# Whole 128x128 products outside column tiling, a narrower memory update, and a newly planned order in a two-layer attention and GEGLU kernel

## The chip, the cores and the metric

The kernel runs on one core of one Trainium2 chip. A core has five engines that work side by side: PE (matrix products, with its weight loads shown apart as PEld), ACT (activations), DVE (vector), POOL (GpSimd) and SP (here it only issues transfers). The metric is the device time of one execution in microseconds, as a median over runs.

## The reference

Two layers, each an attention block with a compressive memory followed by a GEGLU block, with the same weights in both layers. x is 2048 x 512, 32 heads of 16, four segments of 512 rows, hidden width 1792, all bf16.

```python
x = x + _A_ref(_layernorm(x), wq, wk, wv, wo, beta)
x = x + _B_ref(_layernorm(x), w_gate, w_up, w_down)     # and both once more

# _A_ref, for each segment s in order (q, k, v of that segment; M, z start at zero)
logits = einsum('bhqd,bhkd->bhqk', qs, ks) * scale + mask      # causal within the segment
a_dot = einsum('bhqk,bhkd->bhqd', softmax(logits), vs)
pq = phi(qs)                                                   # phi(t) = t + 1 if t > 0 else exp(t)
num = einsum('bhld,bhde->bhle', pq, M)
den = einsum('bhld,bhd->bhl', pq, z)[..., None] + 1e-06
o = g * num / den + (1.0 - g) * a_dot                          # g = sigmoid(beta), per head
M = M + einsum('bhld,bhle->bhde', phi(ks), vs)
z = z + einsum('bhld->bhd', phi(ks))
# ... then o @ wo

# _B_ref
gelu(x @ w_gate) * (x @ w_up) @ w_down
```

## The kernel before, in words

**Work.** There are eight rounds k = 0 to 7: four segments of the first layer, then four of the second. A round normalizes its 512 rows (bn_stats on DVE, the scale on POOL, xn on DVE) and turns them to xnT, by a DMA transpose, or on PE through "ident" for a few tiles (`turn_item`). Then PE makes q, k and v; the scores; the products of the exponentials with the values; the memory terms; the output projection (wo); and the three GEGLU products (wg_sb, wu_sb, wd_sb). Everything PE writes goes to one PSUM tile, `big`, of eight banks of 512 columns. A "product" is one contraction over 128 rows, of up to 512 columns, into 128 output partitions.

**Modes of the array.** PE's array is used in three ways. *Rows*: the scores, four instructions side by side that each contract over 32 partitions (a head's 16, or 32 with the other half zeroed) and write four banks (L1422). *Columns*: four instructions side by side that each contract over 128 partitions and write 32 output partitions. The products of exponentials (`pt`) and values (`vaug`, `vS`) use it because the four heads have different data (L1118), and before the change every other product after the start uses it too, with the same moving data four times (`product`, L655). *Whole*: one instruction over the full array; before the change only the first warm-up products (L553) and the first transposes (L753) are whole. Each instruction is a weight load and a matmul, so a product is eight instructions in columns and two as a whole.

**A score step** is four banks of scores (`visit`), one ACT exponential over the four (`pt`, L1492), causal masks on POOL (L1465), and later a *flush*: the products of `pt` and values in column mode, whose result DVE transposes, divides and transposes back (L1146 to L1161). There are 145 steps. For the first 64 keys and queries of each 128-row diagonal tile a shared form, `kS` (L817) and `vS` (a transfer on SP, L889), packs two heads into one tile.

**Memory.** phi(q) and phi(k) come from an exponential on ACT and two steps on DVE (L923 to L957); phi(k) is turned by a DMA transpose (`phik<-e`). The update (`upd_item`) sums phik x vaug over the segment's four tiles for four blocks of eight heads: 16 products of 128 columns, into a 128 x 128 block per eight heads, of which only the eight 16 x 16 diagonal blocks are M. DVE adds that to `macc` and multiplies it with the block mask `bd` into `mblk` (L1057, L1073). The reading products are `zcols,phiq` (8 columns, the denominator) and `mblk,phiq` (128 columns, the numerator); the quotient `am` goes back by a DMA transpose (`amT<-am`).

**GEGLU.** The gate's result goes to `gel` either through ACT's GELU straight from PSUM, or for the first RAW of the 14 tiles as a copy, on which ACT then runs GELU over GELU_TILES tiles at once (L1274). DVE multiplies with the up product (L1309); the down product is added to x on DVE (L1219). Rounds 0 and 7 treat their rows in two halves, so that their gate and up products are 256 columns wide.

**The order.** The order of every engine is fixed when the program is built. A loop at the end of the kernel holds clocks for all engines (`Clocks`, with a cost per product, 0.108 us for a change of mode, and a simple clock for the loads) and picks, step by step, a score step, a flush, the next product of an open item, or, if nothing is ready, a filler product on `warm` whose result is not read. Which item comes first follows from due times and slacks, in tables of numbers (`DUE`, `BIAS`, `TUNING`, `CHANGES`, the last by stretches of 8 us). On the chip each engine runs its list in order and waits with semaphores, so a late instruction holds all that is listed behind it on that engine.

Of the kernel before, what the change touches and what calls it, by code (L numbers as in the profile page):

```python
# [36 lines left out]
V_FIRST = -0.1406  # L37
WG_GAP, WU_GAP, WD_GAP = 1.1751, 1.964, 2.2
# [7 lines left out]
HALF_DUE = -0.0614  # L46
# [4 lines left out]
WO, WG, X2, WU, X3, WD = 8.92, 8.8357, 9.3414, 26.0, 59.6338, 50.0  # L51
# [3 lines left out]
GELU_TILES = 2  # L55
RAW = 7
QK_DUE = 0.6083
E_Q = -0.5755
E_K = 1.0635


PIECE_SLACK = 2.4403
# [14 lines left out]
DUE = {"wo": 0.9072, "gate": 1.0383, "up": 1.341, "down": 2.1385, "upd": 0.3142, "mem": -0.0606, "v": -0.0049}  # L77
DUE_STEP = {"gate": 0.0081, "up": 0.0201, "down": 0.0554}
BIAS = {
    **{("qk", k): d for k, d in {0: 0.6366, 1: -0.4157, 2: 0.0872, 3: 0.0468, 4: 0.1308, 5: -0.6926, 6: 0.341, 7: 0.1923}.items()},  # L80
    **{("mem", k): d for k, d in {0: -0.207, 1: -0.081, 2: -0.1962, 3: 0.5227, 4: 0.8136, 5: -0.0693, 6: -0.6952, 7: 0.185}.items()},
    **{("down", k): d for k, d in {0: 0.3399, 1: 0.5019, 2: -0.0456, 3: -0.5138, 4: -0.6002, 5: 0.0995, 6: -0.0146, 7: -0.2413}.items()},
    **{("upd", k): d for k, d in {0: 1.4259, 1: 0.8971, 2: -0.1168, 3: 1.283, 4: -0.1814, 5: 0.6044, 6: 0.1034, 7: 1.0768}.items()},
    **{("v", k): d for k, d in {0: -0.3587, 1: 0.46, 2: -0.4336, 3: 2.2572, 4: -0.1536, 5: -1.113, 6: -0.5383, 7: 0.1758}.items()},
    **{("wo", k): d for k, d in {0: -0.1308, 1: 0.6124, 2: -1.1607, 3: -0.6612, 4: -0.5868, 5: -1.3174, 6: 0.2871, 7: -0.2375}.items()},
    **{("gate", k): d for k, d in {0: 0.5854, 1: -0.059, 2: -0.7641, 3: -0.6794, 4: -0.8448, 5: 0.349, 6: -0.5712, 7: -0.7185}.items()},
    **{("up", k): d for k, d in {0: -0.2823, 1: 0.018, 2: -0.1402, 3: -0.3188, 4: -0.0282, 5: -0.0777, 6: -0.2846, 7: 0.3301}.items()},
# [5 lines left out]
    8.0: {"ADD": -17.428, "AHEAD": -0.005, "CAP": 5, "DIRECT": -14.575, "EAGER": 1, "EXP_SLACK": -5.116, "FIRST": -12.912, "FLUSH_WAIT": 9.26, "KB_FIRST": 1.044, "KB_SLACK": 5.078, "KS_FIRST": 3.677, "PHI_SLACK": 9.086, "SCALES": -12.366, "SOON": 0.419, "TURNED": -10.958, "X_NORM": 0.107, "down": -0.264, "gate": -0.13, "qk": -0.178, "up": 0.131, "upd": -0.423, "v": 0.893, "wo": -0.005},  # L93
    16.0: {"ACT_EVICT": -1.716, "ADD": -15.287, "AHEAD": 0.315, "CAP_FREE": 4, "EXP_SLACK": -2.291, "E_SLACK": 11.836, "GELU_SLACK": 0.422, "H_NORM": -12.256, "KB_SLACK": 0.3, "KS_SLACK": 8.888, "MASK_STEP": 0.443, "PHI_SLACK": 3.266, "QUAD": 1, "SCALES": -14.004, "X_NORM": 0.549, "gate": -0.366, "mem": 0.376, "qk": 0.34, "up": -0.311, "upd": -0.413, "v": -0.056},
    24.0: {"ACT_EVICT": 1.44, "CAP_FREE": 4, "DIRECT": -15.128, "EAGER": 1, "E_SLACK": 10.283, "FIRST": -12.109, "FLUSH_WAIT": 14.141, "GELU_SLACK": -0.282, "H_NORM": -13.364, "KB_SLACK": 0.694, "KS_SLACK": 5.286, "PHI_SLACK": 0.4, "SOON": 0.354, "X_NORM": 0.705, "down": 0.382, "gate": -0.53, "mem": 0.434, "qk": 0.414, "v": 0.047, "wo": 0.796},
    32.0: {"ACT_EVICT": 1.686, "ADD": -13.497, "AHEAD": 0.174, "CAP": 3, "CAP_FREE": 6, "EAGER": 0, "EXP_SLACK": 0.685, "E_SLACK": 11.451, "FLUSH_WAIT": 13.243, "GELU_SLACK": -0.725, "KB_FIRST": -1.682, "KS_FIRST": 10.752, "MASK_STEP": 0.471, "MEM_SLACK": 2.767, "PHI_SLACK": 1.429, "QUAD": 0, "SCALES": -12.323, "TURNED": -9.789, "X_NORM": 0.549, "down": 0.592, "gate": -0.755, "mem": -0.285, "wo": -0.005},
    40.0: {"ACT_EVICT": 2.537, "AHEAD": 0.152, "DIRECT": -15.882, "EXP_SLACK": -2.179, "E_SLACK": 12.429, "FLUSH_WAIT": 14.141, "GELU_SLACK": -0.767, "H_NORM": -13.609, "KB_SLACK": 1.429, "KS_FIRST": 6.764, "MEM_SLACK": 2.596, "PHI_SLACK": 4.309, "QUAD": 1, "SCALES": -14.004, "X_NORM": 0.622, "mem": -0.479, "qk": -0.3, "upd": -0.012, "wo": 1.011},
    48.0: {"AHEAD": -0.043, "CAP": 5, "CAP_FREE": 4, "DIRECT": -17.12, "FIRST": -10.627, "GELU_SLACK": 0.029, "KB_SLACK": 0.694, "KS_FIRST": 11.509, "MASK_STEP": 0.139, "MEM_SLACK": 4.617, "PHI_SLACK": 4.307, "QUAD": 1, "SCALES": -14.713, "SOON": 0.173, "mem": -0.412, "qk": -0.299, "upd": -0.805, "v": 0.391},
    56.0: {"ACT_EVICT": 3.045, "ADD": -13.348, "EXP_SLACK": -2.607, "E_SLACK": 11.451, "FIRST": -8.214, "FLUSH_WAIT": 10.746, "GELU_SLACK": -0.767, "KS_FIRST": 13.703, "MASK_STEP": 0.327, "MEM_SLACK": 4.065, "PHI_SLACK": 3.783, "QUAD": 1, "SOON": 0.293, "TURNED": -10.962, "X_NORM": -2.154, "down": 0.561, "gate": -0.36, "mem": -0.457, "qk": -0.363, "up": 0.131, "upd": -1.138, "v": 0.541, "wo": -0.786},
    64.0: {"ACT_EVICT": 1.495, "ADD": -13.677, "AHEAD": 0.164, "KB_SLACK": 1.66, "KS_FIRST": 12.054, "KS_SLACK": 6.956, "MASK_STEP": 0.416, "MEM_SLACK": 4.617, "PHI_SLACK": 12.047, "QUAD": 0, "SCALES": -14.004, "SOON": 0.507, "TURNED": -9.034, "X_NORM": 0.0, "down": 1.162, "gate": -0.726, "upd": -1.362, "v": -0.146, "wo": -1.126},  # L100
    72.0: {"ACT_EVICT": 1.417, "CAP": 5, "CAP_FREE": 6, "EAGER": 0, "EXP_SLACK": -6.38, "E_SLACK": 9.522, "FIRST": -7.036, "H_NORM": -13.913, "KB_FIRST": -1.775, "KB_SLACK": 0.777, "KS_FIRST": 15.351, "MASK_STEP": 0.22, "MEM_SLACK": 5.407, "SCALES": -11.012, "SOON": -0.293, "mem": -0.412, "v": 0.004, "wo": 0.934},
# [57 lines left out]
    536.0: {"AHEAD": 0.262, "FLUSH_WAIT": 8.259, "PHI_SLACK": 3.033, "X_NORM": 0.605, "gate": 0.339, "v": -0.058},  # L159
    544.0: {"ADD": -9.41, "CAP": 5, "DIRECT": -10.972, "H_NORM": -15.619, "KS_FIRST": 10.365, "KS_SLACK": 2.926, "SCALES": -12.181, "SOON": -2.104, "up": 0.0, "upd": 0.734},  # L160
    552.0: {"ACT_EVICT": 1.638, "ADD": -13.506, "EAGER": 0, "E_SLACK": 4.952, "MEM_SLACK": 4.517, "SCALES": -15.328, "X_NORM": 0.0, "down": 0.219, "qk": 0.076, "wo": 0.009},
    560.0: {"CAP_FREE": 4, "DIRECT": -13.0, "KS_SLACK": 5.566, "MEM_SLACK": 5.723, "QUAD": 1, "gate": 0.339, "upd": 0.26},
    568.0: {"mem": 0.212, "upd": 0.26, "wo": -0.274},
}

# [145 lines left out]
class Clocks:  # L311
# [3 lines left out]
    SMALL = 0.033  # L315
    SWITCH = 0.108
    STEP, PART = 0.226, 0.012

    def __init__(self):
        self.pe = 0.0  # L320
        Engine.port.clear()
# [1368 lines left out]
```

## Time and profile before

| | |
|---|---|
| runs | 551.22, 551.36, 552.73 us; median 551.36 |
| profiled execution | span 552.0 us from the first to the last instruction |
| PE busy | 538.8 us, 13,694 matmuls |
| DVE, ACT, POOL busy | 438.7, 414.8, 233.8 us |
| mean granted PE clock | 1.000 |
| read from and written to HBM | 9.71 MB, 2.10 MB |

The profile is that of one execution. A row of the timeline has the start and the duration in us, the engine, the line, the operation, the tiles (out<-in), the shape and how many instructions it merges; in brackets stands the idle time before it and what ended it. "issue" is idle time for which the profile shows no awaited event. A matmul's duration is its whole passage (0.38 us at 512 columns), and several overlap, so the distance between starts tells what one costs. A grouped row has busy time, mean duration in ns, then the idle time before. Rows of the transfers have the size and the median time from issue to landing.

### The profile page before, as it was taken

The numbers are of one execution on the slowest core, as the hardware profiler recorded it, in microseconds if no ns is written. First come the engines' busy times: TensorE is split into PE (matmuls) and PEld (weight loads), VectorE is DVE, ScalarE is ACT, GpSimd is POOL, SyncE is SP. The second block draws the span as 40 slices with busy tenths as digits, with TensorE's granted clock in tenths as the row PEclk, the third lists the DMA queues.
The fourth block names the chain that finished last, engine by engine and source line by source line (L and its number), as shares of the span: only waits on it lengthen the run. The fifth ranks groups of instructions, "written<-read, shape, count | busy, mean of one in ns | idle before, by whom it ended". The sixth has DMA issues, their size and how long they took to land.

```text
span 552.0 us, 29849 instructions
## 1 busy us (share of the span) xinstructions
PE 538.8 (98%) x13694; PEld 294.1 (53%) x13694; DVE 438.7 (79%) x836; ACT 414.8 (75%) x376; POOL 233.8 (42%) x417
## 2 busy tenths in 40 slices
PE   8999899899999999999999999999999999999997
PEld 4445664664454444554444444445454555545994
DVE  7998789889997998589896967489869797588152
ACT  3899879888999877978989687958968855960600
POOL 6459025367438243824383444165562433111000
PEclk9999999999999999999999999999999999999999
DMA  8765626003400223201514020322253004010001
GB/s 256 186 143 121 174 49 95 6 13 61 91 14 2 46 48 51 42 12 34 71 22 61 12 41 13 41 52 32 32 98 61 4 4 99 12 14 22 23 5 40
DMA packets 69775, 30.39 MB, mean 55 GB/s; under 512 B 55120, under 2 KB 69200, under 8 KB 69648
## 3 DMA queue, kind: packets, MB, share of 16 engines
q1 hardware_dynamic: 69504, 28.46, 26.0%
q8 instruction: 107, 1.75, 1.3%
q14 instruction: 20, 0.16, 0.1%
q10 hardware_dynamic: 144, 0.01, 0.0%
HBM read 9.71 MB, written 2.10 MB: 21 GB/s over the span
## 4 chain that ended last, share of the span: by engine, by line
PE 79%; DVE 11%; DMA 3%; ACT 2%; issue 2%; POOL 2%; ACTq 0%; DVEq 0%; POOLq 0%
PE big L655 67%; PE big L1422 7%; PE big L1118 5%; ACT pt L1492 2%; DVE st L678 2%; DVE xn L714 1%; DVE x_sb L1219 1%; DMA xnT<-xn 1%; DVE byq L1146 1%; DVE e L949 1%; DMA amT<-am 1%; DMA phik<-e 1%; DVE ab L1154 1%; DMA x_sb<-in_A_x_dram 1%; POOL pt L1465 1%
## 5 line engine op out<-in xcount | busy, mean ns | idle before, releaser
L1492 ACT ACTIVATE pt<-big 128x2048 bf16<-128x2048 f32 (+1 forms) x147 | 272.7, 1856 | 73.3 <-PE big L1422 65.3
L1465 POOL TENSOR_SCALAR_AFFINE_SELECT pt<-pt 64x256 bf16<-64x256 bf16 (+4 forms) x296 | 146.1, 520 | 238.8 <-ACT pt L1492 235.7
L1309 DVE TENSOR_TENSOR gel<-gel,big 128x512 bf16<-128x512 bf16 x112 | 75.1, 682 | 41.4 <-PE big L655 39.6
L655 PE MATMUL big<-xnT,wu_sb 128*32 128x512 bf16 (+1 forms) x2240 | 105.8, 337 | 2.0 <-issue 2.0
L655 PE MATMUL big<-xnT,wg_sb 128*32 128x512 bf16 (+1 forms) x2240 | 105.5, 337 | 1.0 <-DVE am L1004 0.9
L655 PE MATMUL big<-wd_sb,gel 128*32 128x512 bf16 (+2 forms) x1848 | 105.1, 373 | 0.0
L655 PEld LDWEIGHTS <-wu_sb 128*32 128x32 bf16 x2240 | 58.3, 97 | 36.1 <-issue 5.1
L655 PEld LDWEIGHTS <-wg_sb 128*32 128x32 bf16 x2240 | 57.7, 97 | 35.6 <-issue 6.1
L655 PEld LDWEIGHTS <-gel 128*32 128x32 bf16 x1848 | 47.0, 97 | 43.2 <-issue 4.2
L1219 DVE TENSOR_TENSOR x_sb<-x_sb,big 128x512 bf16<-128x512 bf16 (+1 forms) x65 | 43.1, 667 | 28.2 <-PE big L655 28.2
L1146 DVE STREAM_TRANSPOSE byq<-big 128x512 f32<-128x512 f32 x64 | 45.2, 706 | 8.2 <-PE big L1118 7.1
L1118 PE MATMUL big<-pt,vaug 128*32 128x64 bf16 (+5 forms) x1152 | 44.9, 263 | 0.3 <-issue 0.2
L678 DVE BATCH_NORM_STATS2 st<-x_sb 128x6 f32<-128x512 bf16 x60 | 40.5, 675 | 0.2
L1274 ACT ACTIVATE gel<-big 128x512 bf16<-128x512 f32 x64 | 35.1, 603 | 3.9 <-PE big L655 3.9
L655 PE MATMUL big<-xnT,wq_sb 128*32 128x512 bf16 (+1 forms) x528 | 34.8, 374 | 2.3 <-DMA xnT<-xn 2.0
L655 PE MATMUL big<-xnT,wk_sb 128*32 128x512 bf16 (+2 forms) x528 | 34.6, 373 | 0.4 <-issue 0.4
L655 PE MATMUL big<-wo_sb,aT 128*32 128x512 bf16 x512 | 32.3, 380 | 0.2
L655 PE MATMUL big<-wv_sb,xnT 128*32 128x512 bf16 x512 | 32.0, 380 | 0.0
L817 POOL TENSOR_SCALAR kS<-kf,maskA 128x256 bf16<-128x256 bf16 x28 | 30.4, 1085 | 3.5 <-PE big L1422 2.6
L714 DVE TENSOR_SCALAR xn<-x_sb,mv,rs 128x512 bf16<-128x512 bf16 x64 | 28.4, 489 | 2.5 <-POOL rs L701 1.5
L817 POOL TENSOR_SCALAR kS<-kf,maskB 128x256 bf16<-128x256 bf16 x28 | 29.7, 1060 | 0.5
L1118 PE MATMUL big<-pt,vS 128*32 128x64 bf16 x960 | 27.9, 193 | 0.7 <-DVE xnT L646 0.7
(99 smaller groups left out, 643.8 us busy)
## 6 DMA issues: line engine op xcount, KB each, us to landing
vS<-vaug SPq DMA_DIRECT2D x16, 136.0 KB, 3.0
out_dram<-x_sb SPq DMA_DIRECT2D x15, 128.0 KB, 2.5
wg_sb<-in_B_w_gate_dram SPq DMA_DIRECT2D x8, 224.0 KB, 6.0
wu_sb<-in_B_w_up_dram SPq DMA_DIRECT2D x8, 224.0 KB, 4.1
kB<-kf SPq DMA_DIRECT2D x28, 64.0 KB, 2.9
wd_sb<-in_B_w_down_dram SPq DMA_DIRECT2D x7, 256.0 KB, 5.2
x_sb<-in_A_x_dram SPq DMA_DIRECT2D x3, 512.0 KB, 6.5
xnT<-xn SPq DMA_TRANSPOSE x48, 3.2
```

The source lines that it names most:

```text
L655: nc.tensor.matmul(out[r], lhsT=lhsT[:, r], rhs=rhs, start=start, stop=stop, tile_position=(0, 32 * c))
L678: nc.vector.bn_stats(out=self.st6[:, 0, :], in_=x_sb[:, self.tt0 + j, :])
L714: eng.tensor_scalar(out=xn[:], in0=x_sb[:, self.tt0 + j, :], scalar1=self.mv[:, j, 0:1], scalar2=self.rs[:, j, :], op0=ALU.subtract, op1=A ...
L817: eng.tensor_scalar(out=kS[:, b, :, :, u], in0=self.kf[:, b, :].rearrange("p (t h c) -> p t h c", h=2, c=Q)[:, :, 0, :], scalar1=(maskA, m ...
L1118: nc.tensor.matmul(ps()[32 * j:32 * j + 32, q0 + shift:q1 + shift], lhsT=va[:, ki, values_of(va, b, p, j)], rhs=step["pt"][:, j, c0:c0 + q ...
L1146: nc.vector.transpose(out=self.byq[:, c], in_=ps()[:])
L1219: ck.dve.post(ck.made(), slack, (0.683 - 0.00104 * (D - width), lambda: nc.vector.tensor_tensor(out=xt, in0=xt, in1=ps()[:, 0:width], op=A ...
L1274: return lambda: nc.scalar.activation(out=out(), in_=in_(), func=ACT.Gelu_apprx_tanh)
L1309: ck.dve.post(ck.made(), NORMAL, (0.683, lambda: nc.vector.tensor_tensor(out=hidden(g, h), in0=hidden(g, h), in1=banked(ps), op=ALU.mult), ...
L1422: nc.tensor.matmul(big[:, got[j], c0:c0 + q1 - q0], lhsT=lhsT, rhs=a.q[rows, b, q0:q1], start=True, stop=True, tile_position=(32 * j, 0))
L1465: nc.gpsimd.affine_select(out=v, in_=v, pattern=[[0, m], [by, size]], compare_op=ALU.is_ge, fill=0.0, base=by - 1, channel_multiplier=-1)
L1492: 0.172 + 0.000832 * width * len(banks_of), lambda g=g, st=st: nc.scalar.activation(out=pt[:, g, 0:width], in_=st, func=ACT.Exp, scale=SCA ...
```

## The change

Seven things change.

1. `product` issues one whole 128 x 128 instruction pair unless the array is in column mode already, in which case it stays with four column tiles. So the products behind a score step are whole until the next flush or update, and the products behind those are in columns until the next score step. The transposes of `turn_item` become whole transposes into a bf16 PSUM tile.
2. The memory update uses column tiles with different moving data: each tile of 32 key columns gets the 32 value columns of the same two heads. The block becomes 128 x 32 instead of 128 x 128 for eight heads, `macc` and its additions shrink to a quarter, and the spread to `mblk` is done where `bd` is applied.
3. The planner counts PE's instructions and holds its PE clock where a block of 256 would not have been fetched yet.
4. In round 0 `kS` and `vS` are filled for the second half of the tiles only, the ones in use there.
5. GELU runs over single raw tiles (GELU_TILES 1 instead of 2) and RAW is 8 instead of 7.
6. The transposes' eviction costs 0.4 instead of 0.673 in the plan, and the start is entered in whole mode.
7. All numbers of the tables are new, so the order is new on every engine.

```diff
-WO, WG, X2, WU, X3, WD = 8.92, 8.8357, 9.3414, 26.0, 59.6338, 50.0
+WO, WG, X2, WU, X3, WD = -29.5388, 1.4725, -54.0783, 41.3648, 47.6149, 53.9526
...
-GELU_TILES = 2
-RAW = 7
+GELU_TILES = 1
+RAW = 8
...
-DUE = {"wo": 0.9072, "gate": 1.0383, "up": 1.341, "down": 2.1385, "upd": 0.3142, "mem": -0.0606, "v": -0.0049}
+DUE = {"wo": 1.6259, "gate": 0.1383, "up": 2.6751, "down": 3.6683, "upd": -0.1049, "mem": -2.1806, "v": 0.1361}
...
+    BLOCK, ENTRY, AHEAD = 256, 192, 64
+    FETCH, BEHIND = 3.8, 2.0
...
+    def count(self, n):
+
+        self.issued += n
+        if self.issued >= self.BLOCK * self.asked + self.ENTRY - self.AHEAD:
+            self.asked += 1
+            self.landed.append(max(self.landed[-1], self.pe) + self.FETCH
+                               + min(self.BEHIND, max(0.0, self.dma - self.pe)))
+        if self.issued >= self.BLOCK * self.block + self.ENTRY:
+            self.pe = max(self.pe, self.landed[self.block])
+            self.block += 1
...
-    macc = cst.tile([P, 4, P], F32, name="macc")
+    macc = cst.tile([P, 4, 32], F32, name="macc")
...
     def product(out, lhsT, rhs, start=True, stop=True):
 
+        if ck.mode != "columns":
+            ck.tiling("whole")
+            ck.count(2)
+            nc.tensor.matmul(out, lhsT=lhsT, rhs=rhs, start=start, stop=stop)
+            return
+        in_columns(out, lhsT, [rhs] * 4, start, stop)
+
+    def in_columns(out, lhsT, rhs, start=True, stop=True):
         ck.tiling("columns")
+        ck.count(8)
         for c in range(4):
             r = slice(32 * c, 32 * c + 32)
-            nc.tensor.matmul(out[r], lhsT=lhsT[:, r], rhs=rhs, start=start, stop=stop, tile_position=(0, 32 * c))
+            nc.tensor.matmul(out[r], lhsT=lhsT[:, r], rhs=rhs[c], start=start, stop=stop, tile_position=(0, 32 * c))
...
+            ps = Psum((P, KT, P), BF16)
+
+            def turn(kt):
+                ck.tiling("whole")
+                ck.count(2)
+                nc.tensor.transpose(ps()[:, kt, :], xn()[:, kt * P:(kt + 1) * P], ident[:])
...
                 def copy(b, u, eng):
+                    t = slice(0 if k else TPS // 2, TPS)
                     eng.tensor_scalar(
-                        out=kS[:, b, :, :, u], in0=self.kf[:, b, :].rearrange("p (t h c) -> p t h c", h=2, c=Q)[:, :, 0, :],
+                        out=kS[:, b, t, :, u], in0=self.kf[:, b, :].rearrange("p (t h c) -> p t h c", h=2, c=Q)[:, t, 0, :],
...
+                ts = slice(0 if k else TPS // 2, TPS)
...
-                            out=vS[u:P:2, :, c], in_=self.vaug[0:Q, :, c]),
+                            out=vS[u:P:2, ts, c], in_=self.vaug[0:Q, ts, c]),
...
-                product(psm()[:, b, :], self.phik[:, j, b * P:(b + 1) * P],
-                        by_head(self.vaug)[:, j, 4 * b:4 * b + 4, :, 0:DH], c == 0, c == n_mm - 1)
+                in_columns(psm()[:, b, :], self.phik[:, j, b * P:(b + 1) * P],
+                           [by_head(self.vaug)[:, j, 4 * b + i, :, 0:DH] for i in range(4)], c == 0, c == n_mm - 1)
...
-                    return lambda: nc.vector.tensor_tensor(out=made[0][:], in0=src()[:], in1=bd[:].unsqueeze(1).to_broadcast([P, 4, P]), op=ALU.mult)
+                    return lambda: nc.vector.tensor_tensor(
+                        out=made[0][:].rearrange("p b (i c) -> p b i c", c=32), in0=src()[:].unsqueeze(2).to_broadcast([P, 4, 4, 32]),
+                        in1=bd[:].rearrange("p (i c) -> p i c", c=32).unsqueeze(1).to_broadcast([P, 4, 4, 32]), op=ALU.mult)
...
-    ck.pe, ck.mode, ck.dve.free = 11.4, "columns", 12.0
+    ck.pe, ck.mode, ck.dve.free = 11.4, "whole", 12.0
```

How the order moves is shown at three places. A row has the line, the operation and the tiles, and for PE the output partitions and columns of one instruction; equal rows in a row are left out at the dots.

The first is PE in round 0, where a score step of that round is followed by up products (`wu_sb`). Before, four column instructions per product:

```order
L1422 LDWEIGHTS kB_130
L1422 MATMUL big<-q,kB_130 128x192
L655 LDWEIGHTS wu_sb
L655 MATMUL big<-xnT,wu_sb 32x256
...
L655 LDWEIGHTS phiq
L655 MATMUL big<-zcols,phiq 32x8
```

And now, at a score step of the same form:

```order
L1452 LDWEIGHTS kB_130
L1452 MATMUL big<-q,kB_130 128x192
L671 LDWEIGHTS wu_sb
L671 MATMUL big<-xnT,wu_sb 128x256
...
L1452 LDWEIGHTS kf
L1452 MATMUL big<-q,kf 128x256
```

The up products are one instruction pair each and 19 of them stand in front of the next score step; the denominator's products (`zcols`) have moved behind them.

The second is PE at the memory update of round 0. Before:

```order
L655 LDWEIGHTS wk_sb
L655 MATMUL big<-xnT,wk_sb 32x512
L655 LDWEIGHTS phik
L655 MATMUL big<-vaug_132,phik 32x128
...
L655 LDWEIGHTS wq_sb
L655 MATMUL big<-xnT,wq_sb 32x512
```

And now:

```order
L1452 LDWEIGHTS kB_130
L1452 MATMUL big<-q,kB_130 128x256
L680 LDWEIGHTS phik
L680 MATMUL big<-vaug_132,phik 32x32
...
L680 LDWEIGHTS wk_sb
L680 MATMUL big<-xnT,wk_sb 32x512
```

The update's products are 32 columns wide and follow a score step at once; the k products behind them stay in column tiles, because the update has put the array in column mode.

The third is SP, which issues the loads and the DMA transposes, from the last loads of `wu_sb` to the transposes of round 3's xnT. Before:

```order
L498 DMA wu_sb<-in_B_w_up_dram 128x896 x2
L612 DMA_TRANSPOSE phik<-e 128x4x128 x2
L498 DMA wd_sb<-in_B_w_down_dram 128x2x512
L612 DMA_TRANSPOSE phik<-e 128x4x128
L498 DMA wd_sb<-in_B_w_down_dram 128x2x512 x4
L498 DMA x_sb<-in_A_x_dram 128x4x512
L498 DMA wd_sb<-in_B_w_down_dram 128x2x512 x2
L612 DMA_TRANSPOSE phik<-e 128x4x128
L612 DMA_TRANSPOSE amT<-am 128x4x128
```

(behind these come four kB and two vS transfers, three more amT and then xnT). And now:

```order
L514 DMA x_sb<-in_A_x_dram 128x4x512
L514 DMA wu_sb<-in_B_w_up_dram 128x896 x2
L628 DMA_TRANSPOSE phik<-e 128x4x128
L514 DMA wu_sb<-in_B_w_up_dram 128x896
L514 DMA wd_sb<-in_B_w_down_dram 128x2x512
L514 DMA wu_sb<-in_B_w_up_dram 128x896
L514 DMA wd_sb<-in_B_w_down_dram 128x2x512 x6
L628 DMA_TRANSPOSE xnT<-xn 128x4x128 x4
```

x of segment 3 and the last wu pieces stand in one row of loads, the last wu piece behind a wd piece; round 3's xnT follows the six wd loads and stands ahead of all amT transposes.

206 lines of the change are left out of this document (103 added, 103 removed).

## The prediction

> **What bounds the kernel now.** I read the page first: the span, the busy times, and the shares of the chain of work that ended last.
>
> ```profile
> span 552.0 us, 29849 instructions
> PE 538.8 (98%) x13694; PEld 294.1 (53%) x13694; DVE 438.7 (79%) x836; ACT 414.8 (75%) x376; POOL 233.8 (42%) x417
> PE 79%; DVE 11%; DMA 3%; ACT 2%; issue 2%; POOL 2%; ACTq 0%; DVEq 0%; POOLq 0%
> ```
>
> PE is the bound: 98% busy and 79% of the chain. But "busy" counts overlapping ends, so I took the spacing of starts from the timeline of PE instead (start, duration, line, operation, tiles, count).
>
> ```profile
> 197.10 0.82 PE L655 MATMUL big<-wv_sb,xnT 128*32 128x512 bf16 x12
> 197.75 0.40 PE L655 MATMUL big<-mblk,phiq 128*32 128x128 bf16 x16
> 197.98 0.60 PE L655 MATMUL big<-wo_sb,aT 128*32 128x512 bf16 x8
> 66.14 0.69 PE L655 MATMUL big<-zcols,phiq 128*32 128x8 bf16 x64
> 66.66 0.30 PE L655 MATMUL big<-xnT,wu_sb 128*32 128x256 bf16 x4
> 68.71 1.06 PE L655 MATMUL big<-xnT,wu_sb 128*32 128x256 bf16 x32 [1.75 <-issue]
> ```
>
> Four column instructions are one product. Three products of 512 columns take 197.75 - 197.10, 0.216 us each; four of 128 columns 197.98 - 197.75, 0.057 us each; sixteen of 8 columns 66.66 - 66.14, 0.033 us each. 512 columns in 0.216 us is one column per 0.42 ns: **the column tiles already keep the array full**, and a whole product of the same width has nothing to win there. What is left is the switching between modes and the time in which PE stands still. A switch shows here:
>
> ```profile
> 200.79 1.04 PE L655 MATMUL big<-wo_sb,aT 128*32 128x512 bf16 x16
> 201.76 0.40 PE L1422 MATMUL big<-q,kB 32*128 32x320 bf16 x8
> 202.09 0.38 PE L1118 MATMUL big<-pt,vaug 128*32 128x448 bf16 x4
> 6.46 0.40 PE L753 MATMUL big<-ident,xn 128*128 128x128 bf16 x4
> 6.79 0.40 PE L655 MATMUL big<-warm 128*32 128x512 bf16 x4
> ```
>
> Columns to rows: 0.97 us to the next start, less four products at 0.216 = 0.11. Rows to columns: 0.33, less 0.22 for 320 + 192 columns (at the price of 512) = 0.11. Whole to columns: 0.33, less four transposes at 0.057 = 0.10. I take 0.10 for every switch. PE's own waits are few:
>
> ```profile
> PE big L655 <- issue: 2.3, 3, 1.7
> PE big L655 <- DMA xnT<-xn: 2.0, 2, 1.2
> PE big L1422 <- ACT pt L1492: 1.0, 2, 0.7
> PE big L655 <- DVE am L1004: 0.9, 1, 0.9
> ```
>
> **The change part by part.** Counts are from the instruction orders; prices from rows.
>
> 1. *Array time.* The memory update (96 products, the row below) goes from 128 to 32 columns. No row has 32 columns; 8 and 128 bound it, 0.033 and 0.057. At 0.42 ns a column 32 would fill 0.013, less than even the 8 columns take, so the 0.033 holds: 96 x (0.057 - 0.033) = -2.3 us, and 0 at the other bound. The fillers, products on "warm" issued where the plan has nothing else, go from 42 to 36: -6 x 0.216 = -1.3. All other products keep their widths.
>
> ```profile
> L655 PE MATMUL big<-vaug,phik 128*32 128x128 bf16 x384 | 7.3, 225 | 0.1
> L655 PE MATMUL big<-warm 128*32 128x512 bf16 x168 | 11.6, 380 | 0.0
> ```
>
> 2. *Switches.* Both kernels have 145 score steps. Before, everything else is in columns, so a step costs two switches: 294 with the start. Now a product behind a score step is whole and the pt products are in columns: 81 steps are entered from whole, 64 from columns; 119 are left to whole, 26 to columns; 40 whole-to-columns and 2 back: 332. That is **38 more**, +3.8 us. Whole-to-rows and rows-to-whole stand nowhere in this trace free of a data wait. All three kinds that do lie at 0.10 to 0.11, so I bound the 242 that touch whole mode by 0.09 and 0.115, which is 2.4 us down and 3.6 up on the sum.
>
> 3. *Whole products themselves.* 1,739 products become whole, and 48 transposes. The four transposes at 6.46 are whole, each with its own load of 128 columns of weights, and run at the same 0.057 us as column tiles do; at 256 and 512 columns there is more time to hide the load. The one narrower kind are 48 of the 96 zcols products (8 columns): between 0.033 (columns) and 0.057 (whole, 128 columns) each, so 0 to +1.1; I take the middle, +0.5.
>
> The Trainium skill speaks against this part: "TensorE: Matmul & The Clock Gate", section "Back-to-back issue gap", gives about 81 ns per product for a stream of weight load and product at 128 columns. By that the 79 mblk products and 48 transposes would cost 127 x 0.024 = 3.0 us more. The trace's whole transposes do not show it, and the sum goes by the trace.
>
> 4. *Instruction fetch.* PE's instructions fall from 27,390 to 16,620 rows of the order.
>
> ```profile
> q8 instruction: 107, 1.75, 1.3%
> 63.38 0.43 PE L655 MATMUL big<-xnT,wk_sb 128*32 128x512 bf16 x4
> 64.16 0.81 PE L655 MATMUL big<-xnT,wk_sb 128*32 128x512 bf16 x9 [0.35 <-issue]
> 72.01 0.23 PE L1118 MATMUL big<-pt,vS 128*32 128x64 bf16 x8
> 72.44 0.52 PE L1118 MATMUL big<-pt,vaug 128*32 128x256 bf16 x16 [0.20 <-issue]
> 75.65 0.29 PE L1422 MATMUL big<-q,kB 32*128 32x64 bf16 x8
> 76.17 0.49 PE L655 MATMUL big<-xnT,wu_sb 128*32 128x256 bf16 x9 [0.22 <-issue]
> ```
>
> Queue 8 moved 107 blocks: 27,390 / 107 = 256 instructions each, 16 KB. The first products behind the standstills at 64.16, 68.71, 72.44 and 76.17 are rows 2750, 3006, 3262 and 3518 of the order: exactly 256 apart. So these waits on nothing visible are **PE waiting for its next block of instructions**. Starts tell how long: 0.56 (64.16 - 63.38, less 0.22), 1.94, 0.37 and 0.30, and by the same reckoning 0.3 at 115 and 0.2 at 59: 3.7 us in all. They fall where 256 instructions last only 2.6 to 4.2 us (the sum of the product prices above and of the switches from one such row to the next) and loads are under way. With two instructions for a whole product instead of eight, I reckoned every block of the new order in the same way: one of 64 lasts 2.5 us (rows 3006 to 3262, the narrow memory update of segment 1 and its neighbours), every other 3.9 us or more, and those under 4.2 come late, after the loads. I leave that one 0.7, between nothing and the longest (1.94): -3.0 us, between -1.8 and -3.7.
>
> 5. *Transfers.* Two waits of PE that stand close together, and the loads' times to landing:
>
> ```profile
> 97.27 0.40 PE L1422 MATMUL big<-q,kB 32*128 32x64 bf16 x8 [0.73 <-ACT pt L1492]
> 98.83 0.83 PE L655 MATMUL big<-xnT,wq_sb 128*32 128x512 bf16 x12 [1.16 <-DMA xnT<-xn]
> wd_sb<-in_B_w_down_dram SPq DMA_DIRECT2D x7, 256.0 KB, 5.2
> wu_sb<-in_B_w_up_dram SPq DMA_DIRECT2D x8, 224.0 KB, 4.1
> ```
>
> The xnT at 98.83 is that of segment 3. On SP its four transposes now stand ahead of all amT transposes instead of behind four, so this wait should go: -1.2. But six wd loads now stand directly in front of them, and a new order may wait elsewhere: between 0 and -1.2, I take -0.6. The wait on pt at 97.27 and that on am (0.9) I keep; nothing in the order speaks to them.
>
> 6. *ACT and DVE.* GELU over single raw tiles: 54 instructions instead of 28.
>
> ```profile
> L1274 ACT ACTIVATE gel<-gel 128x1024 bf16<-128x1024 bf16 x20 | 21.4, 1069 | 0.0
> L1274 ACT ACTIVATE gel<-gel 128x512 bf16<-128x512 bf16 x8 | 5.3, 658 | 0.0
> L647 ACT ACTIVATE kf<-big 128x512 bf16<-128x512 f32 x21 | 12.7, 604 | 1.1 <-PE big L655 1.0
> L1492 ACT ACTIVATE pt<-big 128x2048 bf16<-128x2048 f32 (+1 forms) x147 | 272.7, 1856 | 73.3 <-PE big L1422 65.3
> 100.00:150.00 50.00, 49.63 (x1492) 30.56 (x1485) 44.23 (x82) 44.52 (x42) 26.34 (x44) 1.00 0.26 46
> ```
>
> 54 x 0.65 is 35 us against 26.7; six fewer GELUs read PSUM (-3.6) and ACT makes four more evictions (+2.4): about +7 us on ACT. It lies beside PE: before the exponentials ACT waited 65.3 us for scores. Where the cover is thin, 100 to 150 us (ACT 44.5 of 50), its share is about 2 us; the exponentials are what is late next, and PE would wait up to those 2. I take 0. DVE loses a few us (the update's and the transposes' evictions, the halved kS) and the vS loads of segment 0 are halved; neither ends a wait of PE here, so 0. At the start three switches go (-0.3, counted above), but the rows of x set the pace there, so the next wait takes it: +0.3.
>
> Sum: -2.3 - 1.3 + 3.8 + 0.5 - 3.0 - 0.6 + 0.3 = **-2.6 us** on the profiled 552.0, so a span of 549.4. The median of the runs, 551.36, lies 0.6 below the profiled span; I carry that over: **548.8 us**.
>
> **The rivals.**
>
> *A, the forecast:* 548.8, its own range 546 to 551.5 (the switches' bounds, the fetch's, the zcols').
>
> *B, fewer instructions bring nothing:* the standstills are some other disturbance of the busy DMA, and stay: -2.6 + 3.0 = +0.4, 551.8. The 256-row distance speaks against it. The Trainium skill is on its side: "Runtime: NRT & Kernel Launch", section "Instruction fetch mechanics", has blocks of 16 KB and 256 instructions, as this trace has, but calls the cost mostly hidden; the 1.75 us at 68.71 was not.
>
> *C, the new order also waits less for data:* the two DMA waits (2.0), pt (1.0) and am (0.9) all go, 3.3 more than the 0.6 I took, and the switches touch their lower bound (-2.4): 543.1. For it: these waits are few and in named places. Against: the plan's view of DMA and ACT is the old one.
>
> *D, slower through the late loads:* before, the last wu loads were issued by 47 us and the up products of segment 0 began at 64.8 (SP's and PE's timeline).
>
> ```profile
> 46.25 1.05 SPq L498 DMA_DIRECT2D wu_sb<-in_B_w_up_dram  x2
> 64.81 0.84 PE L655 MATMUL big<-xnT,wu_sb 128*32 128x256 bf16 x24
> ```
>
> Now two wu loads stand behind x and a phik transpose, the last behind a wd piece, while up begins 2 us of array time earlier. PE's order is fixed, so PE would stand at the first up product, with the score steps queued behind it and ACT idle for them. Price: one load's 4.1 to 5.2 us and one exponential's 1.9 (the pt row) behind it, some 6: 555. It decides once the last wu load lands later than about 62 us. Against it: issued at 46.9 and landed 4 us later, the load lay some 14 us ahead.
>
> *E, slower through the weights:* after a switch a whole product must first load all 128 columns with nothing to hide it, 97 ns by the row below. 121 switches into whole x 0.097 = 11.7: 560.5. The transposes at 6.46 start with their load, which speaks against it.
>
> ```profile
> L753 PEld LDWEIGHTS <-xn 128*128 128x128 bf16 x16 | 0.9, 97 | 1.4 <-DVE xn L714 1.4
> ```
>
> **How the numbers follow.** A 0.55, B 0.14, C 0.14, D 0.11, E 0.06. About 0.3% (1.65 us) is what a measurement of this kernel can tell from none, so faster is below 549.7 and slower above 553.0. A lies below in three of four cases (0.41), inside in most others (0.12), above in 0.02; C is faster; B is inside but for a little; D and E are slower. Faster 0.55, same 0.25, slower 0.20. The range, 543.5 to 555, takes in most of C and D and leaves out E; the forecast alone would have 546 to 551.5.
>
> **What would show it.** Queue 8 at about 65 blocks and hardly an "issue" wait in PE's waits (step 4); whole products of 512 columns 0.216 us apart, of 128 columns 0.057 (step 3; 0.08 would prove it wrong); about 0.10 us from whole to rows and back (step 2; 0.2 would be E); the vaug,phik products 0.033 apart (step 1); no DMA wait at the segment-3 wq product (step 5); ACT busy about 422 us, and PE's waits on pt no longer than 1.0 us in all (step 6). A wait at the first wu or wd product of segment 0 would be D. The forecast is wrong if waits for data, above all between 40 and 160 us, grow by more than the 3.0 us that the fetch gives back.

## The result, and the profile after

The changed kernel took 545.16 us (median of four runs, 545.11 to 545.39) against 552.05 (four runs) for the kernel before: a ratio of 0.9868 with a 95% interval of 0.9844 to 0.9892. The medians lie 6.9 us apart, and the ratio makes it 7.3 us, with an interval of 6.0 to 8.6; the forecast was 2.6 us. The direction and the range held; the size was more than double.

The page of the changed kernel, in the places that answer those shown of the kernel before:

```profile
span 543.4 us, 19037 instructions
PE 528.0 (97%) x8232; PEld 270.9 (50%) x8309; DVE 434.3 (80%) x838; ACT 418.7 (77%) x402; POOL 238.5 (44%) x417
q8 instruction: 65, 1.06, 0.8%
PE 87%; DVE 7%; issue 3%; ACT 2%; POOL 1%; DMA 1%; ACTq 0%; DVEq 0%
L1304 ACT ACTIVATE gel<-gel 128x512 bf16<-128x512 bf16 x54 | 30.9, 646 | 0.0
L1523 ACT ACTIVATE pt<-big 128x2048 bf16<-128x2048 f32 (+1 forms) x149 | 272.8, 1834 | 68.5 <-PE big L1452 63.0
```

PE is the bound as before, now 87% of the chain instead of 79%. Queue 8 fetched 65 blocks instead of 107. ACT is busy 4 us longer, and still waits 63.0 us for scores.

PE's largest waits after the change (waited for: us in total, times, longest):

```profile
PE big L671 <- issue: 5.2, 33, 0.2
PE big L569 <- DVE warm L547: 1.1, 1, 1.1
PE big L1452 <- ACT pt L1523: 1.0, 1, 1.0
PE big L671 <- DVE byq L1176: 0.9, 4, 0.3
PE big L671 <- DVE xnT L662: 0.5, 1, 0.5
```

The transfer waits (2.0 us) and the wait on am (0.9) are gone. The first row, 5.2 us on "issue" in 33 pieces, looks like the standstill that the change was to end, and isn't. PE's and PEld's rows of one such place, between two score steps (L671 is the whole product):

```profile
276.36 2.11 PE L671 MATMUL big<-xnT,wg_sb 128*128 128x512 bf16 x9 [0.16 <-issue]
276.13 1.84 PEld L671 LDWEIGHTS <-wg_sb 128*128 128x128 bf16 x10 [0.21 <-issue]
```

Ten weight loads stand beside nine products; over the whole trace there are 8,309 loads and 8,232 matmul records. A product of 0.216 us whose record is missing behind a score step leaves a gap of 0.16 us in front of the next. With the missing product put back the array goes on without a stop there.

**Where the time went.** I set the start of every product against the price of the one before it (and of the switch, if there was one), as the prediction did for a few. What is left over is start-up (before 12 us), a standstill at a distance of 256 rows in the order, or a wait for data. The two columns "second" are further profiles of the same kernels, taken with the experiments. The rows add up to the last line but for the 1.1 us before the first product.

| us of PE's time | before | second | changed | second | change, first profiles | predicted |
|---|---|---|---|---|---|---|
| products | 498.0 | 498.0 | 494.1 | 494.1 | -3.9 | -3.1 |
| switches (294, 332) | 30.3 | 30.3 | 33.2 | 33.2 | +3.0 | +3.8 |
| start | 4.0 | 4.0 | 4.5 | 4.5 | +0.4 | +0.3 |
| standstills 256 rows apart, no awaited event | 3.7 | 4.6 | 0.0 | 0.9 | -3.7 | -3.0 |
| waits for data | 7.8 | 8.3 | 4.0 | 4.0 | -3.7 | -0.6 |
| half clock | 0.0 | 1.2 | 0.0 | 0.0 | 0.0 | |
| rests under 0.06 each | 3.9 | 4.4 | 3.5 | 3.5 | -0.4 | |
| start of the last product | 548.7 | 551.9 | 540.4 | 541.2 | -8.3 | -2.6 |

Four fifths of the difference between -2.6 and -8.3 stand in three rows: waits for data (3.1 more than predicted) and the products with their switches (1.6 more).

The profiles lie 8.3 us apart on PE (8.6 in their spans), the runs 6.9. In nine of the eleven later profiles an execution's time lies 1.7 to 1.8 us above its span (545.19 for 543.4 here), in the other two 2.0 and 2.8. So the profiled 552.0 was an execution of 553.7 or more, at least 2.3 above the median of the three runs shown. Part of the waits in that profile were its own.

### The profile page after: what moved, and what is told of

Read it like the earlier page. It is cut to its first block, busy times and chain, and to the rows that moved or that the text cites. A ratio compares the mean times of both kernels' runs of the same rounds, so it can differ in the third digit from the quotient of the medians.

```text
span 543.4 us, 19037 instructions
## 1 busy us (share of the span) xinstructions
PE 528.0 (97%) x8232; PEld 270.9 (50%) x8309; DVE 434.3 (80%) x838; ACT 418.7 (77%) x402; POOL 238.5 (44%) x417
## 4 chain that ended last, share of the span: by engine, by line
PE 87%; DVE 7%; issue 3%; ACT 2%; POOL 1%; DMA 1%; ACTq 0%; DVEq 0%
PE big L671 52%; PE big L680 20%; PE big L1452 8%; PE big L1148 7%; ACT pt L1523 1%; DVE xn L739 1%; DVE x_sb L1249 1%; DVE byq L1176 1%; DMA x_sb<-in_A_x_dram 1%; DVE e L976 1%; DVE ab L1184 0%; DVE st L703 0%; DVE st L1537 0%; DVE gel L662 0%; DVE vaug L662 0%
## 5 line engine op out<-in xcount | busy, mean ns | idle before, releaser
L1496 POOL TENSOR_SCALAR_AFFINE_SELECT pt<-pt 64x256 bf16<-64x256 bf16 (+3 forms) x296 | 149.9, 532 | 233.0 <-ACT pt L1523 220.3
L671 PE MATMUL big<-xnT,wg_sb 128*128 128x512 bf16 (+1 forms) x455 | 82.0, 328 | 1.3 <-issue 1.0
L671 PE MATMUL big<-wd_sb,gel 128*128 128x512 bf16 (+2 forms) x331 | 75.0, 370 | 1.7 <-issue 1.4
L671 PE MATMUL big<-xnT,wu_sb 128*128 128x256 bf16 (+1 forms) x340 | 60.1, 324 | 1.1 <-issue 0.6
L671 PEld LDWEIGHTS <-wg_sb 128*128 128x128 bf16 x469 | 43.8, 98 | 31.4 <-issue 4.2
L671 PEld LDWEIGHTS <-gel 128*128 128x128 bf16 x347 | 31.5, 98 | 36.7 <-issue 3.8
L671 PEld LDWEIGHTS <-wu_sb 128*128 128x128 bf16 x351 | 32.5, 98 | 22.2 <-issue 3.8
L680 PE MATMUL big<-xnT,wu_sb 128*32 128x512 bf16 (+1 forms) x836 | 42.7, 356 | 0.0
L1304 ACT ACTIVATE gel<-gel 128x512 bf16<-128x512 bf16 x54 | 30.9, 646 | 0.0
L680 PEld LDWEIGHTS <-wu_sb 128*32 128x32 bf16 x836 | 22.7, 97 | 15.4
L671 PE MATMUL big<-wo_sb,aT 128*128 128x512 bf16 x114 | 28.8, 380 | 0.6 <-issue 0.3
```

The lines of the kernel that those rows point to most:

```text
L671: nc.tensor.matmul(out, lhsT=lhsT, rhs=rhs, start=start, stop=stop)
L680: nc.tensor.matmul(out[r], lhsT=lhsT[:, r], rhs=rhs[c], start=start, stop=stop, tile_position=(0, 32 * c))
L1304: return lambda: nc.scalar.activation(out=out(), in_=in_(), func=ACT.Gelu_apprx_tanh)
L1496: nc.gpsimd.affine_select(out=v, in_=v, pattern=[[0, m], [by, size]], compare_op=ALU.is_ge, fill=0.0, base=by - 1, channel_multiplier=-1)
```

## The experiments

Two theories stood after the result. F: the gain beyond the update and the fillers comes from the fetch of instructions, so it follows the whole products. O: it comes from the new order, whose products wait less, and the whole products only pay switches.

**The changed kernel again**, for the spread.

> The changed kernel, for comparison on the same chip. Both theories: 545.2 us, PE's stalls beyond array time and switches about 12 us in its profile.

545.75 us (six runs, 545.32 to 546.95), ratio 0.9879 (0.9847 to 0.9910). One standstill shows, which the first profile did not have at the same product (65.37 there):

```profile
66.22 1.69 PE L671 MATMUL big<-xnT,wu_sb 128*128 128x256 bf16 x14 [0.79 <-issue]
```

It is row 1726 of the order: 190 behind a multiple of 256, as 2494 to 3518 were before. The block of 256 instructions in front of it is not a short one: by the prices of its products and switches it lasts 5.7 us. The one short block, of 2.5 us up to row 3262, to which the prediction gave 0.7 us, passed without a stop in both profiles. So a short block is not all that it takes.

**The new order, all products in columns.** PE does the same work in the same order with the fetches of before (105 blocks).

```diff
         if ck.mode != "columns":
             ck.tiling("whole")
             ck.count(2)
-            nc.tensor.matmul(out, lhsT=lhsT, rhs=rhs, start=start, stop=stop)
+            for c in range(4):
+                r = slice(32 * c, 32 * c + 32)
+                nc.tensor.matmul(out[r], lhsT=lhsT[:, r], rhs=rhs, start=start, stop=stop, tile_position=(0, 32 * c))
             return
```

> The changed kernel with its order on every engine kept, but every whole product issued as four column tiles again (the transposes on PE stay whole). Counted in the order: 306 switches instead of 332 and zcols products at 0.033 instead of 0.025 us, together -1.3 us. Theory F (PE waits for blocks of 256 instructions where a block is worked off in less than about 3.6 us while loads run): seven blocks in the first 130 us last 2.2 to 3.4 us again, so 3 to 6 us of standstills come back, 256 rows apart: 547 to 550. Theory O (the order alone made the gain, fetch plays no part): 543.9.

551.55 us, ratio 0.9986 (0.9966 to 1.0006): nearly the whole gain is gone. The row of its fetches, and PE's timeline between 52 and 71 us:

```profile
q8 instruction: 105, 1.72, 1.3%
58.33 1.06 PE L673 MATMUL big<-xnT,wg_sb 128*32 128x256 bf16 x32 [1.83 <-issue]
64.53 0.59 PE L682 MATMUL big<-vaug,phik 128*32 128x32 bf16 x56 [2.15 <-issue]
68.26 0.26 PE L1454 MATMUL big<-q,kB 32*128 32x192 bf16 x4 [0.37 <-issue]
```

The changed kernel has not one wait there. The products behind these waits are rows 2238, 2494 and 2750, with 3262, 3774, 5822 and 6078 behind them: every one 190 above a multiple of 256, 6.1 us in all, against 3.7 in the order before. By the reckoning of the table the rest hardly differs from the changed kernel: products 494.5, switches 31.4, waits for data 5.0. F holds, though the time lies some 1.5 us above the range it gave; O falls, over 7 us off. The new order and the narrow update together, without whole products, brought 0.1%, with an interval from 0.3% faster to 0.1% slower.

**The same once more, for its rows.**

> The new order with every product in column tiles, for a second profile. If the standstills are fetches of the next 256 instructions, they stand at the same rows (2238, 2494, 2750, 3262, 3774, 5822, 6078), 5 to 7 us in all, whatever single transfers do; if they are a disturbance by the loads, their rows differ from the first profile's and their sum may be anything from 1 to 7 us.

551.38 us. The same place:

```profile
58.58 1.06 PE L673 MATMUL big<-xnT,wg_sb 128*32 128x256 bf16 x32 [1.82 <-issue]
64.50 0.59 PE L682 MATMUL big<-vaug,phik 128*32 128x32 bf16 x56 [1.88 <-issue]
68.51 0.26 PE L1454 MATMUL big<-q,kB 32*128 32x192 bf16 x4 [0.65 <-issue]
```

Six of the seven rows are the same, 6.4 us in all, and their lengths differ by up to 0.55 us. The rows alone do not prove a fetch, since the loads are issued at the same places in both executions.

The packets of queue 8 in the traces settle it. Ten of the profiles of this document have standstills of 0.1 us and more at these boundaries, 52 in all, and every one ends 1.2 to 1.6 us after a 16 KB block of instructions has landed. Where PE passed a boundary without a stop, the block had landed at least 1.25 us before. Counted with PE's few semaphore instructions, which the rows leave out, all 52 stand 193 to 199 behind a multiple of 256, early and late in the kernel alike. How long PE stands depends on when the fetch begins and on how long the block in front lasts: in the nine stops of over 1 us the block's packet began 1.5 to 3.7 us after PE had passed the boundary before. In the late stops, at 522 us and behind, of up to 0.5 us, it was 0.7 to 1.7 us. All nine long ones lie between 56 and 72 us, where the loads run (in the column kernel the transfers move 329 GB/s between 62 and 66 us); what holds the packet back there is not shown.

**Whole only early, and whole only late.** The same branch by the plan's clock: whole below 125 us and columns behind it, then the reverse.

```diff
         if ck.mode != "columns":
             ck.tiling("whole")
             ck.count(2)
-            nc.tensor.matmul(out, lhsT=lhsT, rhs=rhs, start=start, stop=stop)
-            return
+            if ck.pe < 125.0:       # in the second kernel: >=
+                nc.tensor.matmul(out, lhsT=lhsT, rhs=rhs, start=start, stop=stop)
+                return
+            for c in range(4):
+                r = slice(32 * c, 32 * c + 32)
+                nc.tensor.matmul(out[r], lhsT=lhsT[:, r], rhs=rhs, start=start, stop=stop, tile_position=(0, 32 * c))
+            return
```

> The changed kernel with its order kept, whole products only in about the first 125 us and column tiles from there on. 310 switches instead of 332: -1.4 us. Theories F and O: 543.8, since blocks that last under 3.6 us stand only late, where hardly a load runs. If a short block stalls wherever it stands, 12 of them cost 0.2 to 0.5 us each: 546 to 549.

> The mirror of it: the same order, column tiles in about the first 125 us and whole products from there on. 330 switches, +0.3 us. Theory F: the early standstills come back, as in the kernel with columns throughout: 548.5 to 551.5. Theory O: 545.5.

Whole early: 547.11 us, ratio 0.9895 (0.9857 to 0.9933). Whole late: 552.88, ratio 1.0001 (0.9978 to 1.0024), 1.4 us above the range of F, with 5.8 us of standstills at the rows of the column kernel:

```profile
62.47 0.59 PE L685 MATMUL big<-vaug,phik 128*32 128x32 bf16 x56 [1.60 <-issue]
67.57 0.26 PE L1457 MATMUL big<-q,kB 32*128 32x192 bf16 x4 [1.75 <-issue]
```

So most of what whole products bring is earned in the first 125 us of the kernel. Later they pay switches, yet giving them up there did not collect those: both theories expected whole early at 543.8, 1.4 below the changed kernel, and it came 1.4 to 2 above, in the range given for the case that a short block stops PE wherever it stands (three of the twelve named do). Its six runs fall into two groups, 545.4 to 546.1 and 548.1 to 548.5, and the profile is of a run of the second, so it speaks for that group alone. It shows two reasons. Three standstills of 0.18 to 0.24 us stand 256 rows apart at 522 to 530 us, in the last GEGLU, where the loads are long over. And one wait for data grew (PE's and SP's timelines of whole early, then SP's of the changed kernel):

```profile
142.79 1.05 PE L685 MATMUL big<-xnT,wq_sb 128*32 128x512 bf16 x16 [2.17 <-DVE macc L1107]
137.81 1.22 SPq L628 DMA_TRANSPOSE xnT<-xn  x1
```

```profile
134.84 1.22 SPq L628 DMA_TRANSPOSE xnT<-xn  x1
139.30 1.05 PE L680 MATMUL big<-xnT,wq_sb 128*32 128x512 bf16 x16
141.08 0.25 DVE L1102 TENSOR_TENSOR macc<-macc,big 128x128 f32<-128x128 f32 x1
```

The profile names the macc addition, since it ended last. But in the changed kernel the same product starts 1.8 us before that addition, so it does not wait for it. What it reads is xnT, whose last transpose was issued 3.0 us later in whole early, while PE was only 1.3 us later there. Which of SP's earlier waits made it late I did not follow.

**The parts at the old order.** Three kernels keep the order before and take over whole products, the narrow update, and both.

```diff
+    array = ["whole"]
...
+        if array[0] != "columns":
+            array[0] = "whole"
+            nc.tensor.matmul(out, lhsT=lhsT, rhs=rhs, start=start, stop=stop)
+            return
...                                     # a flush sets "columns", a score step "rows"
```

```diff
-    macc = cst.tile([P, 4, P], F32, name="macc")
+    macc = cst.tile([P, 4, 32], F32, name="macc")
...                                     # and four column tiles, each with its own two heads
-                product(psm()[:, b, :], self.phik[:, j, b * P:(b + 1) * P],
-                        by_head(self.vaug)[:, j, 4 * b:4 * b + 4, :, 0:DH], c == 0, c == n_mm - 1)
+                    nc.tensor.matmul(psm()[r, b, :], lhsT=self.phik[:, j, b * P + 32 * i:b * P + 32 * i + 32],
+                                     rhs=by_head(self.vaug)[:, j, 4 * b + i, :, 0:DH], start=c == 0, stop=c == n_mm - 1,
+                                     tile_position=(0, 32 * i))
```

> The kernel before with its order on every engine kept; a product is whole where the array is not in column tiles. 341 switches instead of 294 and half of the zcols products at 0.025: +3.3 us of array time and switches, no block under 3.6 us in the first 130 us. Theory F: the 3.7 us of standstills go, so 551.2, between 549.5 and 552.5. Theory O (fetch plays no part): 554.9. Where PE, no longer late, runs into data waits instead, F and O meet near 553.

> The kernel before with its order kept and the memory update alone narrowed to 32 columns per tile (column tiles as before): 96 products at 0.033 instead of 0.056, -2.2 us, and DVE's part of the update shorter. Both theories: 549.3. If the update lay in waits anyway: 551.5.

> Both of these in the kernel before, its order kept: +1.4 us of array time and switches against before. Theory F: 549.3 (fetch -3.7); theory O: 552.9. What is left to the changed kernel's 545.2 is then the work of the order and its tables: about 4 by F, about 8 by O.

| order before, with | us | ratio to before | products | switches | standstills at 256 | waits for data |
|---|---|---|---|---|---|---|
| narrow update | 551.37 | 0.9971 (0.9945 to 0.9996) | 495.8 | 30.3 | 4.2 | 7.7 |
| whole products | 550.89 | 0.9955 (0.9932 to 0.9978) | 497.4 | 34.0 | 0.7 | 4.6 |
| both | 550.00 | 0.9937 (0.9913 to 0.9962) | 495.2 | 34.4 | 2.0 | 6.0 |

Beside these the kernel before took 553.35 us (29 runs), and the ratios are to that. The update is worth 0.3%, 1.6 us of the 2.3 predicted, and the interval holds the 2.3. Whole products are worth 0.45%, 2.5 us, though they make 47 switches more (341, +3.8 us). F had expected next to nothing from them (551.2 against 551.36) and O a loss. The standstills among the loads are gone, which pays for most of the switches (3.7 us of standstills before, 0.7 with whole products); the other row that falls is waits for data, from 7.8 to 4.6, and 1.25 us of that is the transfer wait at 97. The 29 runs of before spread over 550.9 to 556.8 us, the 12 with whole products over 550.7 to 551.8. In 15 of the 29 the mean granted clock is below 0.999, and their median is 554.7 against 552.2 of the other 14; none of the 12 shows such a clock, one of the 12 of "both" does, and none of the ten of the changed kernel. So about half of the 2.5 us comes of executions with a stretch at half clock. In the kernel with both one standstill among the loads returned, at row 1730, and three stand in the last GEGLU. From "both" to the changed kernel 0.6 to 0.7% is left, 3 to 4 us: that is the new order once the products are whole, with the smaller parts of the change. Fewer products, the fillers above all (1.1), and fewer switches (1.2) make 2.3 of it in the reckoning; the rest is fewer waits and standstills.

So the parts do not add up. In columns the new order brings nothing measurable to the narrow update (0.9986 with it, 0.9971 without, and the intervals overlap); with whole products it brings 0.6 to 0.7%. In columns the fetch stops PE among the loads for 6.1 to 6.4 us in the new order and for 3.4 to 3.7 in the old one, which uses up what it saves elsewhere; whole products take nearly all of these stops away.

**The new code with the old tables.**

> The changed code with all tables of numbers as before, so the order is planned from the old numbers. 191 fillers instead of 42 in the order it gives, 29 us of array time more than before: both theories about 580. It tells whether numbers found for one plan hold for another.

588.68 us. The planner of the change, given the numbers of before, finds an order with 191 fillers, which take 191 x 0.216 = 41 us:

```profile
L669 PE MATMUL big<-warm 128*128 128x512 bf16 x92 | 23.4, 380 | 0.3 <-DVE gel L1337 0.3
L678 PE MATMUL big<-warm 128*32 128x512 bf16 x396 | 23.2, 379 | 0.0
```

(92 whole, 396 / 4 = 99 in columns; the changed kernel has 36 in all.) It shows only that the tables belong to the code. The planner's fetch count is another matter: with its cost set to zero and the new tables, the order comes out the same, row for row, on every engine. That part of the change moved nothing here.

**The kernel before, once more.**

> The kernel before once more, unchanged, for a second profile. If the waits of PE for data are a property of its order, the second execution shows the same ones: 0.9 us at 46, 0.8 at 96, 1.25 at 97, 0.9 at 154, 1.4 at 413 to 414, 0.4 at 457, some 7.7 us in all, and the standstills without a cause at rows 2494 to 3518 and 5822. If part of them is chance, the two waits that the narrow update alone no longer showed or still showed tell which: the transfer wait at 97 (1.2 us) is missing, the one on am at 413 stands, and the span is 1 to 2 us shorter than 552.0.

552.91 us, ratio 0.9995 (0.9955 to 1.0035), with single runs from 551.1 to 558.9; its profiled execution had a span of 555.0, 3.0 longer than the first and not 1 to 2 shorter. Three rows of PE's timeline, two rows of its waits, and a window of 2 us (the third number from the end is the granted clock):

```profile
49.45 1.28 PE L655 MATMUL big<-xnT,wq_sb 128*32 128x512 bf16 x16 [2.88 <-DMA xnT<-xn]
50.48 1.96 PE L655 MATMUL big<-xnT,wk_sb 128*32 128x512 bf16 x16
52.19 0.68 PE L655 MATMUL big<-ident,xn 128*32 128x128 bf16 x16
PE big L655 <- DMA xnT<-xn: 2.9, 1, 2.9
PE big L655 <- DVE am L1004: 0.4, 1, 0.4
50.00:52.00 2.00, 2.00 (x28) 0.95 (x21) 0.00 (x0) 0.60 (x1) 2.00 (x3) 0.53 0.78 183
```

The wait of 0.9 us at 46 is 2.9 here, and the wait of 1.2 us at 97, on which step 5 rested, is not there; the narrow update at the same order of SP did not show it either. The waits on ACT's pt (0.80, at 96 in the first profile) and on DVE (0.87, at 154) are the same to 0.01 us. The wait on am behind 413 repeats less closely: 0.4 here and 0.9 before in the profile's rows, 0.9 and 1.4 by the spacing of starts. So two waits on engines repeat, a third does in part, and the two on transfers differ from one execution to the next. At the same place the changed kernel turns its xnT on PE and waits 0.5 us for DVE:

```profile
48.45 0.38 PE L671 MATMUL big<-xnT,wq_sb 128*128 128x512 bf16 x1 [0.51 <-DVE xnT L662]
```

Its ten runs lie between 545.1 and 547.0.

## Why the prediction was right in direction and wrong in size

*Step 1, array time: right.* Sixteen products of the update run in the 0.49 us from 59.42 to 59.91, 0.031 us each (0.033 predicted), and the fillers are 36.

```profile
59.42 0.66 PE L680 MATMUL big<-vaug,phik 128*32 128x32 bf16 x64
59.91 1.06 PE L680 MATMUL big<-xnT,wk_sb 128*32 128x512 bf16 x16
```

*Step 2, switches: 0.8 too dear.* The count was right, and so was 0.10 for whole to rows (0.096) and rows to whole (0.102, over 84 places). But the before's columns to rows is the dearest kind, 0.107, and whole to columns (0.093) the cheapest: 30.3 to 33.2 is +3.0, inside the bounds that the prediction gave (2.4 less and 3.6 more than its +3.8). A switch costs 0.103 on average before and 0.100 after.

*Step 3, whole products: right at 128 columns and above, wrong in sign at 8.*

```profile
6.82 0.39 PE L778 MATMUL big<-ident,xn 128*128 128x128 bf16 x4
7.04 0.38 PE L671 MATMUL big<-warm 128*128 128x512 bf16 x1
178.00 2.11 PE L671 MATMUL big<-xnT,wu_sb 128*128 128x512 bf16 x9 [0.16 <-DVE byq L1176]
180.03 0.40 PE L1452 MATMUL big<-q,kB 32*128 32x64 bf16 x8
74.75 0.54 PE L671 MATMUL big<-zcols,phiq 128*128 128x8 bf16 x16
75.22 0.29 PE L1148 MATMUL big<-pt,vaug 128*32 128x256 bf16 x4
```

0.22 / 4 = 0.055 us at 128 columns; (2.03 - 0.10) / 9 = 0.214 at 512; (0.47 - 0.09) / 16 = 0.024 at 8. The bounds for the zcols products, 0.033 and 0.057, were wrong because both came from products of other shapes: one whole instruction of 8 columns costs less than four in columns. That is -0.4 instead of +0.5. The Trainium skill, "TensorE: Matmul & The Clock Gate", section "Back-to-back issue gap", has about 81 ns per product at 128 columns with a load each; 55 ns here decides against it. Rival E (weights exposed) falls with the same rows.

*Step 4, fetch: right, and somewhat larger.* -3.7 in the profiles for the -3.0 taken; 65 blocks as predicted. But the rule by which it sized what is left, short blocks among the loads, named the wrong block: the one given 0.7 us never stopped PE, and one of 5.7 us did, in one profile of two. Rival B ("fewer instructions bring nothing") is refuted by the column kernel. The step also treated the standstills of before as a fixed price. They hang on the order: 3.4 to 6.4 us for 105 to 107 blocks.

*Step 5, waits for data: the step that failed.* "Between 0 and -1.2, I take -0.6" became -3.7 in the profiles. The step looked at the one wait at 97, which is gone (-1.2) but was partly chance in that execution. Those kept, as nothing in the order spoke to them, fell too: 413 to 414 (1.4, am), 154 (0.9 to 0.2) and 457 (0.4). The wait on pt only moved, from 97 to 105. That is the mechanism of rival C, in part: it had am and pt gone and 543.1. Against the typical run the gain in waits is smaller: the runs moved by 6.9, and without the waits the rows of the table make -4.6, so about -2.3 is left for them. Of the 4.3 us by which the forecast fell short of the runs, the waits are then 1.7, the products and switches of steps 1 to 3 another 1.6, and the fetch 0.7. The wait at 413 is gone with whole products at the old order, and also in the new order with all products in columns; it stands with the narrow update alone. So either of the two removes it, and how is open. The wait at 457 goes with the new order alone.

*Step 6, ACT: right that it is hidden.* Busy +3.9 instead of +7, at the same number of table loads. One wait of PE hangs on it (ACT's rows, then PE's):

```profile
102.46 1.28 ACT L1523 ACT_TABLE_LOAD   x1
103.75 1.88 ACT L1523 ACTIVATE pt<-big 128x2048 bf16<-128x2048 f32 x1
105.68 0.40 PE L1452 MATMUL big<-q,kf 16*128 16x320 bf16 x8 [1.04 <-ACT pt L1523]
```

A GELU and the table behind it hold the exponential for PE, 1.0 us as before in two pieces.

*Rival D (late wu and wd loads) did not come:* no wait for a load stands at the first up or down product of segment 0.

*The last line of the sum was wrong too.* It carried -0.6 from span to run. The distance was +1.7 to +2.8 in every later profile, so the profiled execution was longer than a typical one, and the sum should have been set against a typical run, with part of its transfer waits taken as luck.

## What to carry to other kernels

Find the standstills that wait for nothing, and look up their rows. Here a fixed distance of 256 instructions, and a block of the instruction queue that had landed 1.2 to 1.6 us before each of them ended, showed instruction fetch. Then fewer instructions per unit of work are worth more than the array time says, but mainly where the fetches begin late, here in the first 125 us. Judge an order together with the instruction count it runs with, since the gains of the two don't add. And take a second profile before pricing a transfer wait: two on engines repeated to 0.01 us, a third measured 1.4 and 0.9, and two on transfers 1.2 and 0, 0.9 and 2.9.

## What the hardware showed that was not expected

- A standstill at a 256-row boundary took up to 2.3 us, and 0.1 to 0.5 us even at 522 to 536 us, long after the last load, in the second profile of before, in whole early and in all three kernels at the order before. Early or late, PE went on 1.2 to 1.6 us after its block had landed.
- Behind the wait of 2.9 us in the second profile of before, the four wk_sb products took 1.71 us (50.48 to 52.19), 0.43 each instead of 0.216, with a granted clock of 0.53 between 50 and 52 us. The trace's clock record has half clock for 3.41 us from 50.13. By the table the stretch cost 1.2 us on top of the wait.
- A whole product of 8 columns took 0.024 us, less than the 0.033 of four column tiles of 8.
- All frequent changes of mode cost nearly the same, from 0.093 us (whole to columns) to 0.107 (columns to rows).
